# Window attention whose order is planned in Python: two step costs of the plan, and a new order of 281 offloaded tiles

## The chip, the cores and the metric

The kernel runs on one core of a Trainium2 chip. Its time is the device time of one execution in microseconds; the time of a kernel is the median of its runs. Five engines of the core work side by side, each through its own list of instructions: TensorE (PE in the profile, with its weight loads as PEld), ScalarE (ACT), VectorE (DVE), GpSimd (POOL) and SyncE (SP), which issues most DMAs. They wait for each other by semaphores only.

## The reference

An image of 224 x 224 positions with 96 channels (bf16) is projected to queries, keys and values. The first 48 channels attend within horizontal stripes of 8 rows, the other 48 within vertical stripes of 8 columns; a stripe has 8 x 224 = 1792 positions, and there are 28 stripes in each direction. The two halves are put side by side and projected by `wo`.

```
qkv = einsum('bhwc,cd->bhwd', x, wqkv)
# first 48 channels: 28 horizontal stripes of 1792 positions
ah = softmax(einsum('bqc,bkc->bqk', qh, kh) * 48 ** -0.5)
oh = einsum('bqk,bkc->bqc', ah, vh)
# last 48 channels: 28 vertical stripes, in the same way, give ov
return einsum('bhwc,cd->bhwd', concat(oh, ov), wo)
```

Nearly all of the work is the 1792 x 1792 scores of each of 56 stripes: their product, their exponential, and their product with the values.

## The kernel before

**Tiling.** Two stripes are worked on at once, in the two halves of TensorE's rows: 28 pairs P, first 14 horizontal, then 14 vertical. The 1792 queries of a pair are cut into four chunks c of 512, 512, 512 and 256. A tile is 128 keys of both stripes by the 512 queries of a chunk (in the last chunk 256 keys by 256 queries): 128 x 1024 scores in two PSUM banks. A pair has 14 + 14 + 14 + 7 = 49 tiles, the kernel 1372.

**The way of a tile.** Most tiles are ACT tiles: a score step on TensorE (`qk_fn`, matmuls on L670) writes two banks, ScalarE takes the exponential into a buffer PT (L888), and a value step on TensorE (`pv_fn`, L696) multiplies it with the values and sums in a bank per chunk. The others, here called offloaded tiles, get their exponential from DVE and POOL, by a square and a bit pattern. Their score step (`s_fn`, L683) goes to banks 6 and 7. In the short kind DVE moves the scores out (L1189), POOL squares them (L1105), TensorE computes the scores again (L683), and DVE combines both (L1199). In the long kind DVE copies once (L1188) and POOL does the rest (L1108 to L1111), with one score step. Which kind a tile becomes is decided by the planned backlog of POOL (L1187). ACT's score steps use the two bank pairs 0/1 and 2/3, and in some places the pair 6/7 as a third.

**Other work of TensorE.** Between these, TensorE projects keys and queries (L435) and values (L481) of the next pair, and finishes chunks: a finishing step (`fin_fills` from L513, matmuls on L530 for horizontal and L566 for vertical pairs) multiplies up to five blocks of 64 positions (or 128) with `wo`, and DVE and POOL scale and add.

**Two modes.** The planner distinguishes mode A (score steps of both kinds and finishing steps; contraction over 64 rows at most) from mode B (value steps and projections; contraction over 96 to 128 rows). Going from one to the other costs TensorE time.

**What sets the order.** No engine chooses anything at run time. `Sched` and the functions `step_pe`, `step_dve` and `step_pool` simulate the engines in Python while the program is built, with fixed costs from the top of the file (L25 to L35): a step of TensorE takes `D_MM` = 0.216 us, ACT comes every `P_ACT` = 0.9167 us, a change from A to B costs `SWT["AB"]` = 0.124 and from B to A 0.097. `commit` (L136) adds `W_PE` = 0.021 to the second step after a change; it keeps in `S.run` how many steps have followed the first of a run (0 for a lone step). `pe_switch` (L867) is the place where a change is charged; if the last step of mode A was a finishing step it adds `W_FIN`. The finishing steps are given 0.026 us for each of their n blocks (L547, L597). From these costs the planner knows at each moment how long it has until ACT's next score step is due (`slack` in `step_pe`), and puts value steps, projections, finishing and offloaded steps into it. The simulated order then becomes the engines' lists; `settle` (L1259) puts in the waits that are needed. So the costs change no instruction, only the order.

`HOW` (L43) holds choices for each pair: a string of three digits, the numbers of offloaded tiles in the first three chunks; a number that sets how early the next pair's projections are due; and four words of twelve hexadecimal digits, a word per chunk, which `RULES` (L75) reads as thresholds for `step_pe`, `step_dve` and the kinds of tile. The first digit, for one, is the number of value steps (`B1`, L1065) for which there must be room before the planner leaves mode A:

```
win = slack - SW_AB - SW_BA
nn = min(npv + (1 if fb else 0), int((win + how()[8]) / D_MM + 1e-6))
if nn >= B1 or ...
```

The eighth digit allows an ACT tile to take the third bank pair (L992).

Of the kernel before, what the change touches and what calls it, by code (L numbers as in the profile page):

```python
# [24 lines left out]
SWT = {"AB": 0.124, "AC": 0.124, "BA": 0.097, "CA": 0.10, "BC": 0.098, "CB": 0.108}  # L25
SW_AB, SW_BA = SWT["AB"], SWT["BA"]
D_ACT, P_ACT, M_ACT, SEMA = 0.904, 0.9167, 1.0175, 0.053
D_MM, L_MM, L_PV, L_FILL = 0.216, 0.465, 0.44, 0.215
W_PE, W_FIN = 0.021, 0.06
SEMD, SEMP, SELF, SEMX = 0.15, 0.12, 0.19, 0.05  # L30
D_P1, D_SQ, D_ADD = 1.14, 1.852, 0.0019
D_TS, D_TW = 1.125, 1.28
# [8 lines left out]


HOW = [  # L43
    ("023", 11, "242426002612 394226102014 324227102012 327227100012"),
    ("464", 7, "336319113442 331319113442 331319113442 335319113444"),
    ("323", 12, "521219112723 539418120834 539418120834 434418120234"),
    ("354", 10, "399238123332 399238123343 569429010920 569429110923"),
    ("334", 2, "383429102532 383429102532 383425102532 383135102532"),
    ("334", 9, "383135102932 546317021634 562226102334 5a7326002334"),
    ("342", 7, "5a7326102314 5a7325002311 568429003732 568429003730"),  # L50
    ("446", 5, "568429003733 433316102523 566439000041 566439000021"),
    ("233", 1, "475325003244 475325023241 475325123243 479325121243"),
    ("444", 0, "479325101243 479225101224 479225101221 479225101222"),
    ("224", 0, "479225100222 2a2327102823 2a5327102823 2a5317002823"),
    ("424", 3, "245217002823 245217002843 245217022843 245217020843"),
    ("544", 8, "381329000711 381329000911 247236022532 4a8425113033"),
    ("243", 4, "511318021714 511318021714 511318001724 4a5438023343"),
    ("444", 1, "4a5428023343 4a5436023343 312316012422 312336012422"),
    ("224", 6, "332236012422 372436010422 5a1219103932 521239103932"),
    ("334", 9, "521239002931 521239002932 421239002942 421239002942"),  # L60
    ("443", 2, "369428110343 369428110342 366425110342 273436003342"),
    ("343", 6, "273436001331 273436001423 273436001423 273336001422"),
    ("224", 9, "379316100602 358338000810 222419002813 222419002512"),
    ("342", 5, "232419002542 279339002241 279319002241 522136000512"),
    ("444", 10, "522438000513 3a2329000422 3a7119100312 453417001532"),
    ("443", 8, "453417021530 449415012722 489415012022 542214103644"),
    ("334", 9, "542214103641 388426102621 388426100622 201438102334"),
    ("334", 12, "201418103334 201418123333 466216100841 318216113541"),
    ("323", 2, "318217112542 218218112542 541117111741 5a9436000032"),
    ("333", 4, "5a9138000032 5a9138002032 333319101722 335319100722"),  # L70
    ("453", 11, "335119100722 5a6316122020 5a6315121020 5a6325101020"),
]
OFF = [[int(d) for d in k] + [0] for k, _, _ in HOW]
TAIL = [t for _, t, _ in HOW]
# [89 lines left out]
def bass_standalone__window_attn_cswin__vision_kernel(  # L164
# [27 lines left out]
    with es:  # L192
# [64 lines left out]
        S = Sched()  # L257
# [255 lines left out]
        def fin_fills(P, fs):  # L513
            b = P % 2
            fills = []
            if ph_of(P) == 0:
                m = P
                hw = WB // 2
                for bc0 in (list(range(0, hw, FS)) + list(range(hw, WB, FS)) if m == 0 else range(0, WB, FS)):
                    n = min(FS, (hw if m == 0 and bc0 < hw else WB) - bc0)  # L520
                    need = chunk_of_col((bc0 + n) * 64 - 1)
                    ri = rcn[0] % NRC
                    rcn[0] += 1

                    def pe_fn(e, bk, bc0=bc0, n=n):
                        bk3 = bk[:, 0:FS * (C + 1)].rearrange("p (s c) -> p s c", s=FS)
                        for s in range(n):
                            bc = bc0 + s
                            for w in range(2):
                                ins = e.matmul(bk3[64 * w:64 * w + 64, s, :],  # L530
                                               lhsT=o_of(P, w, bc),
                                               rhs=woh[64 * w:64 * w + CA, :], start=True, stop=True)
                        return ins

                    def d1(e, bk, n=n, ri=ri):
                        bk3 = bk[:, 0:FS * (C + 1)].rearrange("p (s c) -> p s c", s=FS)
                        return e.reciprocal(rc[ri][:, 0:n], bk3[:, 0:n, C])

                    def d2(e, bk, n=n, ri=ri, bc0=bc0):
                        bk3 = bk[:, 0:FS * (C + 1)].rearrange("p (s c) -> p s c", s=FS)  # L540
                        dst = Ph_sb[:, m, bc0:bc0 + n, :]
                        if m == 0:
                            v = bc0 // hw
                            dst = Ph_sb[:, m, :, :].rearrange("p (a v) c -> p v a c", v=2)[:, v, bc0 - v * hw:bc0 - v * hw + n, :]
                        return e.tensor_tensor(dst, bk3[:, 0:n, 0:C],  # L545
                                               rc[ri][:, 0:n].unsqueeze(2).to_broadcast([128, n, C]), ALU.mult)
                    fills.append((need, fill("A", 0.026 * n, pe_fn,  # L547
                                             ["wo"] + [("OT", b, c) for c in range(chunk_of_col(bc0 * 64), need + 1)],
                                             [(0.1, d1, [], [("rc", ri)], None),
                                              (0.06 + 0.104 * n, d2, [("rc", ri)], ["Ph"], None)],  # L550
                                             [("OT", P, need)], ("fin", P, bc0))))
            else:
                for w in range(2):
                    j = 2 * (P - NPH) + w
                    for k0 in range(0, NKT, fs):
                        n = min(fs, NKT - k0)
                        late = P == NP - 1 and k0 + n == NKT
                        need = chunk_of_col((k0 + n) * 128 - 1)
# [31 lines left out]
                        for s in range(n):  # L590
                            def d2(e, bk, s=s, ri=ri, w=w, kt=k0 + s, j=j):
# [2 lines left out]
                                                              Ph_sb[:, kt, j, :], ALU.mult, ALU.add)  # L594
                            chain.append((0.225, d2, [("rc", ri), "Ph"], [("o", P, w, k0 + s), ("out", P - 2)], None,
                                          (P, w, k0 + s, j)))
                        fills.append((need, fill("A", 0.026 * n, pe_fn,  # L597
                                                 ["wo"] + [("OT", b, c) for c in range(chunk_of_col(k0 * 128), need + 1)],
                                                 chain, [("OT", P, need), ("fin", NPH - 1, 25)], ("fin", P, w, k0))))
            return sorted(fills, key=lambda z: z[0])  # L600
# [112 lines left out]
        mode = ["B"]  # L713
# [117 lines left out]
        for need, f in fin_fills(0, FS):  # L831
            fin_q.append(f)
# [3 lines left out]
        fin_last = [False]  # L836
# [43 lines left out]
        def issue_qka(t, s):  # L880
            tl = act_seq[ia[0]]
            slot = slot_free.pop(0)
            t = pe_switch(t, "A")
            since[0] += 1
            fin_last[0] = False
            S.commit("pe", t, D_MM, L_MM, qk_fn(tl, s), kt_keys(tl), set_keys(s), fresh=set_keys(s),
                     tag=("qk", tl["P"], tl["c"], tl["kts"][0]))
            S.commit("act", 0.0, D_ACT, None, lambda e, s=s, slot=slot: e.activation(  # L888
                PT[slot][:], ps[:, 512 * SETS[s]:512 * SETS[s] + 1024], ACTF.Exp, scale=LN2 / 128.0),
                set_keys(s), pt_keys(slot), fresh=pt_keys(slot))  # L890
# [457 lines left out]
```

## Time and profile before

| | |
|---|---|
| median of 3 runs | 1017.95 us (1017.44 to 1018.09) |
| profiled execution, its own time | 1017.86 us |
| its span, first to last instruction | 1016.0 us |
| granted TensorE clock | 1.000 |
| exponentials on ACT (L888) | 1090 |
| tiles on DVE and POOL, short and long kind | 180 and 102 |
| busy: PE, ACT, POOL, DVE | 98%, 99%, 92%, 91% |

The span leaves out 1.9 us of the execution's own time ahead of the first and after the last instruction. Each matmul's time in the profile contains the time in which it passes through the array, so starts of successive steps, and not lengths, tell how long TensorE needs for one. ACT's instructions overlap in the same way: the distance of their starts is shorter than their length.

### The profile page before, as it was taken

The numbers are of one execution on the slowest core, as the hardware profiler recorded it, in microseconds if no ns is written. First come the engines' busy times: TensorE is split into PE (matmuls) and PEld (weight loads), VectorE is DVE, ScalarE is ACT, GpSimd is POOL, SyncE is SP. The second block draws the span as 40 slices with busy tenths as digits, with TensorE's granted clock in tenths as the row PEclk, the third lists the DMA queues.
The fourth block names the chain that finished last, engine by engine and source line by source line (L and its number), as shares of the span: only waits on it lengthen the run. The fifth ranks groups of instructions, "written<-read, shape, count | busy, mean of one in ns | idle before, by whom it ended". The sixth has DMA issues, their size and how long they took to land.

```text
span 1016.0 us, 31766 instructions
## 1 busy us (share of the span) xinstructions
PE 994.1 (98%) x13833; PEld 401.2 (39%) x13833; DVE 927.0 (91%) x1509; ACT 1005.9 (99%) x1101; POOL 931.8 (92%) x666
## 2 busy tenths in 40 slices
PE   9999999999999999999999999999999999999998
PEld 4434433433343344334334334333443433343343
DVE  7999899889998989899999999889999999999897
ACT  8999999999999999999999999999999999999997
POOL 5999999899999999998999999999889899999993
PEclk9999999999999999999999999999999999999999
DMA  4403203204202311220111221223313033313111
GB/s 87 98 28 65 67 14 65 66 2 79 65 2 65 79 34 34 65 38 13 28 38 23 56 54 25 51 57 65 53 20 62 18 59 55 61 21 57 24 21 37
DMA packets 162877, 47.08 MB, mean 46 GB/s; under 512 B 155895, under 2 KB 162711, under 8 KB 162738
## 3 DMA queue, kind: packets, MB, share of 16 engines
q1 hardware_dynamic: 161762, 44.59, 21.8%
q8 instruction: 108, 1.77, 0.7%
q10 hardware_dynamic: 976, 0.47, 0.2%
q14 instruction: 31, 0.25, 0.1%
HBM read 10.60 MB, written 19.28 MB: 29 GB/s over the span
## 4 chain that ended last, share of the span: by engine, by line
ACT 97%; PE 2%; DVE 0%; issue 0%; DVEq 0%
ACT PT L888 97%; PE ps L696 1%; PE ps L670 1%; PE ps L346 0%; ACT xT_sb L747 0%; PE ps L481 0%; PE ps L731 0%; DVE out_all L593 0%; PE ps L566 0%; PE ps L463 0%; DVE OT_sb L1164 0%; PE ps L435 0%; DVE warm L309 0%; DVE rc L573 0%; DVEq L192 0%
## 5 line engine op out<-in xcount | busy, mean ns | idle before, releaser
L888 ACT ACTIVATE PT<-ps 128x1024 bf16<-128x1024 f32 x1090 | 1001.5, 1078 | 1.3 <-PE ps L670 1.1
L670 PE MATMUL ps<-QT_sb,KT_sb 49*64 49x512 bf16 (+1 forms) x5144 | 446.0, 363 | 15.4 <-ACT PT L888 3.4
L696 PE MATMUL ps<-PT,V_sb 128*49 128x512 bf16 (+1 forms) x3136 | 451.5, 360 | 0.3 <-ACT PT L888 0.2
L1105 POOL TENSOR_TENSOR PT<-qb 128x1024 f16<-128x1024 f32 x180 | 337.8, 1893 | 8.8 <-DVE qb L1189 5.2
L670 PEld LDWEIGHTS ps<-QT_sb,KT_sb 49*64 49x64 bf16 x5144 | 129.3, 103 | 341.6 <-ACT PT L888 315.0
L1189 DVE TENSOR_SCALAR qb<-ps 128x1024 f32<-128x1024 uint16 x180 | 219.9, 1222 | 22.4 <-PE ps L683 20.1
L1199 DVE SCALAR_TENSOR_TENSOR PT<-ps,PT 128x1024 uint16<-128x1024 bf16 x180 | 219.7, 1221 | 17.3 <-PE ps L683 15.9
L696 PEld LDWEIGHTS ps<-PT,V_sb 128*49 128x49 bf16 x3136 | 134.7, 103 | 165.8 <-issue 130.2
L1109 POOL TENSOR_TENSOR PT<-PT 128x1024 f16<-128x1024 f16 x102 | 193.0, 1892 | 5.9
L683 PE MATMUL ps<-QT_sb,KT_sb 50*64 50x512 bf16 x1848 | 181.3, 382 | 1.3 <-DVE V_sb L488 0.2
L1110 POOL TENSOR_SCALAR qb<-PT 128x1024 uint16<-128x1024 f16 x102 | 137.4, 1347 | 8.8
L1108 POOL TENSOR_SCALAR PT<-qb 128x1024 f16<-128x1024 uint16 x102 | 106.5, 1044 | 33.0 <-DVE qb L1188 24.2
L1188 DVE COPY qb<-ps 128x1024 f32<-128x1024 f32 x102 | 124.6, 1221 | 7.9 <-PE ps L683 5.9
L1111 POOL TENSOR_SCALAR PT<-qb 128x1024 uint16<-128x1024 f32 x102 | 106.5, 1044 | 8.3
L451 DVE CAST QT_sb<-ps 128x512 bf16<-128x512 f32 (+1 forms) x111 | 67.6, 615 | 10.2 <-PE ps L435 9.9
L1164 DVE CAST OT_sb<-ps 113x512 bf16<-113x512 f32 x112 | 69.3, 618 | 5.7 <-PE ps L696 4.7
L440 DVE TENSOR_SCALAR_CACHE_REDUCE KT_sb<-ps 128x512 bf16<-128x512 f32 x108 | 65.9, 615 | 1.2 <-PE ps L435 0.6
L683 PEld LDWEIGHTS ps<-QT_sb,KT_sb 50*64 50x64 bf16 x1848 | 52.5, 104 | 33.3 <-DVE PT L1199 6.3
L545 DVE TENSOR_TENSOR Ph_sb<-ps,rc 128x480 bf16<-128x480 f32 (+1 forms) x84 | 52.4, 623 | 2.8
L488 DVE CAST V_sb<-ps 128x480 bf16<-128x480 f32 (+1 forms) x84 | 51.4, 619 | 3.3 <-PE ps L481 2.8
L584 POOL TENSOR_TENSOR out_all<-tmp,Ph_sb 128x480 bf16<-128x480 f32 (+1 forms) x48 | 49.8, 1046 | 3.2 <-DVE tmp L580 2.6
L593 DVE SCALAR_TENSOR_TENSOR out_all<-ps,rc,Ph_sb 128x96 bf16<-128x96 f32 x165 | 40.5, 310 | 1.1
(63 smaller groups left out, 416.2 us busy)
## 6 DMA issues: line engine op xcount, KB each, us to landing
cols_dram<-in_x_dram SPq DMA_DIRECT2D x28, 336.0 KB
out_dram<-out_all SPq DMA_DIRECT2D x387, 24.0 KB, 1.9
xT_sb<-cols_dram SPq DMA_TRANSPOSE x28, 4.6
xT_sb<-in_x_dram SPq DMA_TRANSPOSE x26, 4.6
xT_sb<-ones_dram SPq DMA_DIRECT2D x26, 7.0 KB
Ph_sb<-in_x_dram SPq DMA_DIRECT2D x2, 168.0 KB, 3.7
Ph_sb<-in_x_dram ACTq DMA_DIRECT2D x2, 168.0 KB, 3.9
out_dram<-out_all ACTq DMA_DIRECT2D x5, 24.0 KB, 1.9
```

The costliest lines, as they stand in the source:

```text
L670: ins = e.matmul(bank(SETS[s] + w)[64 * kh:64 * kh + 64, i * t["qs"]:(i + 1) * t["qs"]], lhsT=KT_sb[b][64 * w:64 * w + CA, kt * 128 + 64 * ...
L683: ins = e.matmul(bank(PB0 + w)[64 * kh:64 * kh + 64, 0:512], lhsT=KT_sb[b][64 * w:64 * w + nr, kt * 128 + 64 * kh:kt * 128 + 64 * kh + 64] ...
L696: ins = e.matmul(bank(pb)[64 * w:64 * w + CA, 0:t["qs"]], lhsT=V_sb[b][:, w, kt, :], rhs=PT[slot][:, ca:ca + t["qs"]], start=st and i == 0 ...
L888: S.commit("act", 0.0, D_ACT, None, lambda e, s=s, slot=slot: e.activation(PT[slot][:], ps[:, 512 * SETS[s]:512 * SETS[s] + 1024], ACTF.Ex ...
L1105: return [("pool", (D_SQ, L_SQ, 0.0), lambda e: e.tensor_tensor(y, q, q, ALU.mult), qk, yk)]
L1108: return [("pool", (D_TS, L_TS, LATE_TS), lambda e: e.tensor_scalar(y, lo, 2.0 ** -16, QH, ALU.mult, ALU.add), qk, yk), ("pool", (D_SQ, L_ ...
L1109: ("pool", (D_SQ, L_SQ, 0.0), lambda e: e.tensor_tensor(y, y, y, ALU.mult), yk + ["pser"], yk),
L1110: ("pool", (D_TW, L_TW, LATE_TS), lambda e: e.tensor_scalar(lo, y, 65536.0 * P2, 65536.0 * QC0, ALU.mult, ALU.add), yk + ["pser"], [("q", ...
L1111: ("pool", (D_TS, L_TS, LATE_TS), lambda e: e.tensor_scalar(bits, q, 1.0, 128.0 * (127.0 - SOFF), ALU.mult, ALU.add), qk, yk)]
L1188: S.commit("dve", t, D_P1, D_P1 + SEMD, lambda e: e.tensor_copy(qb[tl["qb"]][:], ps[:, PB0 * 512:(PB0 + 2) * 512]) if tl["whole"] else e.t ...
L1189: qb[tl["qb"]][:], ps[:, PB0 * 512:(PB0 + 2) * 512]) if tl["whole"] else e.tensor_scalar(
L1199: S.commit("dve", t, D_P1, D_P1 + SEMD, lambda e: e.scalar_tensor_tensor(PT[tl["slot"]][:].bitcast(U16), half(BF16, 1), 128.0 * (127.0 - S ...
```

## The change

It has three parts. The score steps of a run: `pe_switch` takes `W_RUN` = 0.0225 us off the cost of a change from A to another mode, if at least one step followed the first one of the run (`S.run` not 0). The finishing steps: each is given 0.03 us more, and `W_FIN` goes from 0.06 to 0.03, so that a finishing step followed by a change costs the same as before apart from `W_RUN`, and one followed by another step of mode A costs 0.03 more. The order: all 28 rows of `HOW` are new; their first strings add up to 281 offloaded tiles, where it was 282.

```diff
-W_PE, W_FIN = 0.021, 0.06
+W_PE, W_FIN, W_RUN = 0.021, 0.03, 0.0225
...
 HOW = [
-    ("023", 11, "242426002612 394226102014 324227102012 327227100012"),
-    ("464", 7, "336319113442 331319113442 331319113442 335319113444"),
...
-    ("453", 11, "335119100722 5a6316122020 5a6315121020 5a6325101020"),
+    ("032", 8, "4a2223101924 322438100622 496417100211 496417100241"),
+    ("335", 6, "496418100243 254318001934 254318001930 254318001930"),
...
+    ("444", 6, "332238101512 332238102512 305327102022 493114003041"),
 ]
...
-                    fills.append((need, fill("A", 0.026 * n, pe_fn,
+                    fills.append((need, fill("A", 0.026 * n + 0.03, pe_fn,
...
-                        fills.append((need, fill("A", 0.026 * n, pe_fn,
+                        fills.append((need, fill("A", 0.026 * n + 0.03, pe_fn,
...
         def pe_switch(t, m):
             if mode[0] == m:
                 return t
-            d = SWT[mode[0] + m] + (W_FIN if mode[0] == "A" and fin_last[0] else 0.0)
+            d = SWT[mode[0] + m] + (W_FIN if mode[0] == "A" and fin_last[0] else 0.0) - (W_RUN if mode[0] == "A" and S.run else 0.0)
```

More of the change, by code (lines that the diff above doesn't have):

```diff
@@ L43 @@
 HOW = [
-    ("023", 11, "242426002612 394226102014 324227102012 327227100012"),
-    ("464", 7, "336319113442 331319113442 331319113442 335319113444"),
[L46 to L70, printed above, removed]
-    ("453", 11, "335119100722 5a6316122020 5a6315121020 5a6325101020"),
+    ("032", 8, "4a2223101924 322438100622 496417100211 496417100241"),
@@ new lines @@
+    ("335", 6, "496418100243 254318001934 254318001930 254318001930"),
+    ("423", 12, "245427002132 245427002124 245427002621 245427002621"),
+    ("334", 10, "245127002622 245127102622 482427000343 482427000313"),
+    ("335", 12, "236128100724 236128000721 236328000731 236328000233"),
+    ("333", 8, "401237100624 401238102624 401228002624 369219101213"),
+    ("443", 10, "369119101213 368319101613 268339101611 268339101614"),
+    ("335", 6, "268329101614 268329101613 268329102621 228328102421"),
@@ new lines @@
+    ("333", 9, "282424001943 282427001943 282427002943 232427002941"),
+    ("535", 10, "232428002943 262418002643 269328100311 269228101333"),
+    ("322", 9, "209218101333 209218100333 209418101333 209418001333"),
+    ("535", 3, "251329102314 251329002314 251219002314 451219002314"),
+    ("324", 12, "4a6226120822 231228101544 231328102544 231328102644"),
+    ("334", 6, "557219112633 555219012633 555419012630 555119002631"),
+    ("324", 12, "585119001631 585119001632 585419001632 585219001632"),
@@ new lines @@
+    ("355", 2, "385219001532 385219001732 585219001232 587219001232"),
+    ("344", 8, "587219001234 431325000911 375335001012 279318101622"),
+    ("323", 5, "279418101622 454328002542 454428001542 454428001542"),
+    ("434", 7, "598218000832 598218000833 598218000833 2a1434110021"),
+    ("324", 10, "345219021641 245219021641 247319021642 463336002423"),
+    ("422", 10, "443236022423 365318112712 365318012722 365418012722"),
+    ("433", 11, "365415012742 334218102913 434218102913 434218002913"),
@@ L72 @@
+    ("424", 8, "225337110041 4a9217000642 4a9217000642 4a9217000642"),
+    ("345", 12, "4a9317002632 4a9317003632 4a9317003634 542428023242"),
+    ("323", 4, "542428003241 316218102911 3a6318102913 3a6318101913"),
+    ("532", 4, "3a6318101413 3a6318101513 3a6318001513 3a2318001743"),
+    ("444", 6, "3a2318001743 302218001743 302238101743 302238101613"),
+    ("444", 6, "332238101512 332238102512 305327102022 493114003041"),
 ]
```

## The prediction

> **What bounds the kernel now.** I began with the page: span, busy shares, the chain that ended last, and the groups. The columns of a group are line, engine, operation, tiles, shapes, count, then busy us, mean ns of one, idle us before them and what ended that.
>
> ```profile
> span 1016.0 us, 31766 instructions
> PE 994.1 (98%) x13833; PEld 401.2 (39%) x13833; DVE 927.0 (91%) x1509; ACT 1005.9 (99%) x1101; POOL 931.8 (92%) x666
> ACT 97%; PE 2%; DVE 0%; issue 0%; DVEq 0%
> L888 ACT ACTIVATE PT<-ps 128x1024 bf16<-128x1024 f32 x1090 | 1001.5, 1078 | 1.3 <-PE ps L670 1.1
> L1105 POOL TENSOR_TENSOR PT<-qb 128x1024 f16<-128x1024 f32 x180 | 337.8, 1893 | 8.8 <-DVE qb L1189 5.2
> L1189 DVE TENSOR_SCALAR qb<-ps 128x1024 f32<-128x1024 uint16 x180 | 219.9, 1222 | 22.4 <-PE ps L683 20.1
> L1199 DVE SCALAR_TENSOR_TENSOR PT<-ps,PT 128x1024 uint16<-128x1024 bf16 x180 | 219.7, 1221 | 17.3 <-PE ps L683 15.9
> L1109 POOL TENSOR_TENSOR PT<-PT 128x1024 f16<-128x1024 f16 x102 | 193.0, 1892 | 5.9
> L683 PE MATMUL ps<-QT_sb,KT_sb 50*64 50x512 bf16 x1848 | 181.3, 382 | 1.3 <-DVE V_sb L488 0.2
> L1110 POOL TENSOR_SCALAR qb<-PT 128x1024 uint16<-128x1024 f16 x102 | 137.4, 1347 | 8.8
> L1108 POOL TENSOR_SCALAR PT<-qb 128x1024 f16<-128x1024 uint16 x102 | 106.5, 1044 | 33.0 <-DVE qb L1188 24.2
> L1188 DVE COPY qb<-ps 128x1024 f32<-128x1024 f32 x102 | 124.6, 1221 | 7.9 <-PE ps L683 5.9
> L1111 POOL TENSOR_SCALAR PT<-qb 128x1024 uint16<-128x1024 f32 x102 | 106.5, 1044 | 8.3
> ```
>
> The kernel looks bound by ScalarE (ACT): its 1090 exponentials fill 1001.5 of 1016.0 us, and the chain gives ACT 97%. But one exponential lasts 1078 ns, and (1001.5 - 1.08) / 1089 gives one start per 0.9187 us: neighbours overlap by 0.16 us, so an exponential that comes up to 0.16 us late leaves no idle time and the page cannot show it. The timeline of ACT can (start, length, count):
>
> ```profile
> 538.76 12.95 ACT L888 ACTIVATE PT<-ps 128x1024 bf16<-128x1024 f32 x14
> 550.52 1.19 ACT L888 ACTIVATE PT<-ps 128x1024 bf16<-128x1024 f32 x1
> ...
> 244.31 1.05 ACT L888 ACTIVATE PT<-ps 128x1024 bf16<-128x1024 f32 x1
> 245.42 1.02 ACT L888 ACTIVATE PT<-ps 128x1024 bf16<-128x1024 f32 x1
> ```
>
> From 538.76 to 550.52 there are 13 starts, 0.9046 us apart: this is what ACT does when its scores are there. From 244.31 to 245.42 it took 1.11 us. Over the kernel 1089 x (0.9187 - 0.9046) = 15.4 us are such hidden lateness: ACT's floor is 1089 x 0.9046 = 985.1 us, and TensorE's order puts 15.4 on top. Who is late? The waits of the weight loads:
>
> ```profile
> PEld ps L670 <- ACT PT L888: 315.0, 875, 0.8
> PEld ps L696 <- issue: 130.2, 522, 0.4
> ```
>
> In 875 places a score step's weights waited for ACT to free its PSUM banks: TensorE is early there. The second row is time between score steps and value steps. So ACT and TensorE take turns as the bound: TensorE waits in most score steps, and in the rest ACT starts late. DVE and POOL are busy 91% and 92%.
>
> **The change, part by part.**
>
> *One tile goes back to ACT.* The first strings of the 28 rows of the order add up to 282 tiles for DVE and POOL before (the page: 180 + 102) and to 281 after; so 1091 exponentials. Cost: one start, 0.9046 us at the floor, 0.9187 at the mean. I take +0.92, since the other 1090 keep the mean too.
>
> *That tile leaves DVE, POOL and TensorE.* A tile of the short kind is two DVE passes (1.22 + 1.22) and one POOL square (1.89), and two score steps; of the long kind one DVE pass, 1.04 + 1.89 + 1.35 + 1.04 = 5.32 of POOL, and one score step. DVE and POOL stand 8 to 9% idle, beside ACT; I cost this at 0, the lower end is one score step's 0.24 us (timeline below, 92.33 to 92.58) twice, -0.5. If that cover were gone, with POOL the bound, it would be up to -5.3; POOL's 84 us of idle time speak against it.
>
> *The new prices.* They cost no instruction; they tell the planner how long TensorE takes, and so decide how much it puts between two score steps. The planner was charging 0.216 for a score step plus 0.124 for the change to value work = 0.340 after any score step, and 0.130 + 0.060 + 0.124 = 0.314 after a finishing step of five blocks. Now, after at least two steps of the score kind, 0.216 + 0.124 - 0.0225 = 0.3175, and 0.160 + 0.030 + 0.124 - 0.0225 = 0.2915. What TensorE does stands in its timeline. I counted all changes from 20 to 1000 us; below are the first and the last of three kinds: a run that ends in an offloaded tile's step (L683, 194 times), one that ends in an ACT tile's step (L670, 229, of them 208 like these), and one that ends in a finishing step of five (76).
>
> ```profile
> 23.65 0.39 PE L683 MATMUL ps<-QT_sb,KT_sb 50*64 50x512 bf16 x4
> 23.96 0.40 PE L696 MATMUL ps<-PT,V_sb 128*49 128x512 bf16 x2
> ...
> 996.67 0.39 PE L683 MATMUL ps<-QT_sb,KT_sb 50*64 50x512 bf16 x4
> 996.98 0.40 PE L696 MATMUL ps<-PT,V_sb 128*49 128x512 bf16 x2
> ...
> 20.36 0.41 PE L670 MATMUL ps<-QT_sb,KT_sb 49*64 49x512 bf16 x4
> 20.70 0.40 PE L696 MATMUL ps<-PT,V_sb 128*49 128x512 bf16 x2
> ...
> 999.06 0.41 PE L670 MATMUL ps<-QT_sb,KT_sb 49*64 49x512 bf16 x4
> 999.40 0.40 PE L696 MATMUL ps<-PT,V_sb 128*49 128x512 bf16 x2
> ...
> 38.96 0.39 PE L530 MATMUL ps<-woh,OT_sb 49*64 49x97 bf16 x10
> 39.27 0.40 PE L696 MATMUL ps<-PT,V_sb 128*49 128x512 bf16 x2
> ...
> 981.04 0.38 PE L566 MATMUL ps<-wov,OT_sb 49*64 49x97 bf16 x10
> 981.35 0.41 PE L696 MATMUL ps<-PT,V_sb 128*49 128x256 bf16 x4
> ```
>
> After L683 the value step starts 0.31 us later (0.3175 is right, 0.340 was too much). After these L670 it is 0.34: the old price was right, the new is too low by 0.0225. After five finishing blocks it is 0.31: again the old price was right, and the new is too low by 0.019. Why the two kinds of score step differ is seen where the run stands in full, beside a score step that is alone:
>
> ```profile
> 86.78 0.41 PE L670 MATMUL ps<-QT_sb,KT_sb 49*64 49x512 bf16 x4
> 87.12 0.40 PE L696 MATMUL ps<-PT,V_sb 128*49 128x512 bf16 x2
> ...
> 92.03 0.38 PE L696 MATMUL ps<-PT,V_sb 128*49 128x512 bf16 x2
> 92.33 0.41 PE L670 MATMUL ps<-QT_sb,KT_sb 49*64 49x512 bf16 x4
> 92.58 0.39 PE L683 MATMUL ps<-QT_sb,KT_sb 50*64 50x512 bf16 x4
> 93.06 0.41 PE L670 MATMUL ps<-QT_sb,KT_sb 49*64 49x512 bf16 x4
> 93.40 0.41 PE L435 MATMUL ps<-xT_sb,w_sb 97*64 97x512 bf16 x2
> ```
>
> An unbroken second step starts 0.24 after the first and is left after 0.31 to 0.32: two cost 0.56, one alone 0.34, so the second adds one step's 0.216 and the change costs the same as after one. The L670 at 93.06 came 0.48 after the L683, not 0.24: it had waited, TensorE had run empty, and it is left like a lone step, after 0.34.
>
> So the prices do three things. (a) Right price, 194 x 0.0225 = 4.4 us: before, this was slack that the plan did not know of; now the plan can fill it. It is a gain for the order only as far as TensorE is the late one: between 0 and -4.4, and I take the middle, -2.2. (b) Too low, 208 x 0.0225 = 4.7 us: value work is planned that early and comes later: 0 to +4.7. These changes stand behind a score step that waited for ACT, where TensorE was early a moment ago, so I take less than the middle, a third, +1.6. (c) Too low after finishing steps, 76 x 0.019 = 1.4: 0 to +1.4, the middle, +0.7. The finishing step's own +0.03 is for those followed by another step of the score kind; there the 0.0225 comes off one step later, 0.0075 are left, and I cost that at nothing; at 53 places it would be 0.4 in either direction.
>
> The Trainium skill, TensorEngine Tiling (Array Packing), Key Properties, says that changing the tiling mode, not just the tile, drains TensorE. By that rule a change would cost the same whatever ran before it. The rows agree for unbroken runs (0.56 against 0.34, one step more) and the rule speaks against a price that depends on the length of the run; what it would make of the sum is the last rival below.
>
> *The new order.* All 28 rows are other choices. The trace of before cannot price them. Bounds: no order goes below ACT's floor (-15.4), and above it the sum has no end in the rows; nearest is the present order, value 0. I read from the strings: the value steps at which the planner leaves score work fall from a mean of 3.58 to 3.13, and the third pair of PSUM banks is allowed to ACT's tiles in 15 of 112 rows instead of 42.
>
> **Sum:** 0.92 - 2.2 + 1.6 + 0.7 = +1.0 us on the profiled execution's 1017.86 (span 1016.0), 1018.9. The median of the runs shown, 1017.95, is 0.1 above it, so the predicted time is 1019.0. Since 0.2% is about what a measurement of this kernel can tell from no change, "same" here is 1015.9 to 1020.0.
>
> **Rivals.**
>
> *The right price pays in full (faster).* All of (a) is won, (b) and (c) vanish in waits for ACT: 0.9 - 4.4 = -3.5, 1014.5. For it: the 875 waits, where TensorE has time; 15.4 us of lateness to take from. Against: it has to win the extra tile back first, so lateness must fall from 15.4 to under 12.4 before it counts as faster.
>
> *More changes between the kinds of work (slower).* A lower bound for leaving score work means more and shorter runs. A pair of changes costs 0.34 - 0.216 = 0.124 one way; the way back is 92.33 - 92.03 - 0.216 = 0.084; together 0.21 us. At half on the path, each added pair is +0.11; from 10 added pairs on, with the +1.0, it is slower by over 0.2%; 25 more (3% of the 790 changes that I counted in that stretch, 263 after a lone step among them) give +3.8, 1021.7. For it: cheaper changes invite it, and TensorE is 98% busy. Against: fewer offloaded tiles, hence one or two score steps less.
>
> *The prices do nothing.* The order is fixed by the strings; the prices shift no step much: only the tile stays, +0.92, 1018.9. It lies within the forecast.
>
> *A change costs the same after every run (slower).* Then 0.0225 is too little after all 194 + 208 + 76 = 478 runs, 10.8 us, half of it on the path: 0.9 + 5.4 = +6.3, 1024.2. This is the drain rule read strictly. The 0.31 after 23.65 and 996.67 speak against it.
>
> **How the numbers follow.** Forecast 0.41 and "the prices do nothing" 0.13, both same; right price in full 0.13, faster; more changes 0.30 and equal changes 0.03, slower. So faster 0.13, same 0.54, slower 0.33. The forecast's own range, with (a) or (b) moved by a quarter of its span (1.1 to 1.2 us), is 1017.8 to 1020.2. To leave out no more than 2 in 10, the range goes down to 1015.4, into the faster case, and up to 1022.2, over most of the case of more changes.
>
> **What would show it.** ACT: 1091 exponentials; a pitch of 0.9187 or a little above is the forecast, under 0.915 is the right price, 0.921 and more the slower cases. TensorE: 0.31 after L683 and 0.34 after an L670 that waited, as now; a changed number here would overturn (a) or (b). More places in the row of L696's loads on "issue" than 522 would show more changes. I am wrong if POOL or DVE, not TensorE, turn out to be what ACT's lateness hangs on, through value steps that wait for offloaded tiles, or if the new order itself, which I set at 0, is better or worse by more than the prices.

## The result and the profile after

The changed kernel takes 1020.36 us (median of 9 runs, 1020.09 to 1020.78), the kernel before 1018.02 on the same chip: ratio 1.0025, 95% interval [1.0017, 1.0034]. That is 1.4 us above the forecast of 1019.0 and just above the forecast's own range of 1017.8 to 1020.2. It lies inside the whole range on record, 1015.4 to 1022.2, which had been drawn wider to take in two rivals. With +2.3 us it is just beyond the 0.2% up to which the forecast said "same", and the interval has that bound in it.

The page of the kernel after (columns as before):

```profile
span 1018.4 us, 31719 instructions
...
PE 991.8 (97%) x13820; PEld 402.9 (40%) x13820; DVE 917.6 (90%) x1468; ACT 1008.1 (99%) x1102; POOL 948.1 (93%) x683
...
ACT 96%; PE 3%; DVE 0%; issue 0%; DVEq 0%
...
L888 ACT ACTIVATE PT<-ps 128x1024 bf16<-128x1024 f32 x1091 | 1003.8, 1067 | 1.4 <-PE ps L670 1.1
...
L1105 POOL TENSOR_TENSOR PT<-qb 128x1024 f16<-128x1024 f32 x177 | 332.3, 1892 | 6.7 <-DVE qb L1189 3.4
...
L1109 POOL TENSOR_TENSOR PT<-PT 128x1024 f16<-128x1024 f16 x104 | 196.8, 1892 | 6.6
```

There are 1091 exponentials and 177 + 104 = 281 offloaded tiles. One start takes (1003.8 - 1.07) / 1090 = 0.9199 us, it was 0.9187. The rows for exponentials grew by 2.3 us: 0.92 is the tile, 1.4 is lateness spread over all starts. TensorE is busy for 2.3 us less than before and the kernel is slower, so the sum of TensorE's work does not explain the difference; what is left to ask is when its score steps come.

The last exponentials, in the timeline of ACT, before and after (the first row is of two instructions):

```profile
1008.83 2.09 ACT L888 ACTIVATE PT<-ps 128x1024 bf16<-128x1024 f32 x2
```
```profile
1011.80 1.17 ACT L888 ACTIVATE PT<-ps 128x1024 bf16<-128x1024 f32 x1
```

They end at 1010.92 and 1012.97: 2.0 of the 2.4 us of span arise up to there, 0.4 after it.

TensorE's timeline of the kernel after, with the last change behind an offloaded tile's step (127 of them from 20 to 1000 us), the first behind an ACT tile's step that had waited (256), and the first behind five finishing blocks (62):

```profile
998.73 0.39 PE L683 MATMUL ps<-QT_sb,KT_sb 50*64 50x512 bf16 x4
999.05 0.40 PE L696 MATMUL ps<-PT,V_sb 128*49 128x512 bf16 x2
...
21.78 0.41 PE L670 MATMUL ps<-QT_sb,KT_sb 49*64 49x512 bf16 x4
22.12 0.40 PE L696 MATMUL ps<-PT,V_sb 128*49 128x512 bf16 x2
...
38.54 0.39 PE L530 MATMUL ps<-woh,OT_sb 49*64 49x97 bf16 x10
38.85 0.40 PE L696 MATMUL ps<-PT,V_sb 128*49 128x512 bf16 x2
```

0.32, 0.34 and 0.31: as in the kernel before. The chip has not changed its prices; the plan has.

**The planner's clock.** Since the order comes from a simulation in the kernel's code, that code has a time for the last exponential as well. It is no measurement, but beside the trace it tells how wrong the prices are in sum. Below, a trace whose last exponential ends before that time is called early, and one that ends after it late. Before, the clock says 1012.22 us and the trace 1010.92: 1.3 early. After, it says 1011.07 and the trace 1012.97: 1.9 late. The distance grows evenly and not in lumps: the first exponential of the kernel after is 0.9 us early, the 500th is on time, the last 1.9 late. So the new plan is 1.15 us better than the old one on paper, with a tile more on ACT, and it loses 3.2 us against its paper. The experiments ask what these 3.2 us are.

### The profile page after: what moved, and what is told of

It reads as the page before. It is cut to its first block, busy times and chain, and to the rows that moved or that the text cites. A ratio compares the mean times of both kernels' runs of the same rounds, so it can differ in the third digit from the quotient of the medians.

```text
span 1018.4 us, 31719 instructions
## 1 busy us (share of the span) xinstructions
PE 991.8 (97%) x13820; PEld 402.9 (40%) x13820; DVE 917.6 (90%) x1468; ACT 1008.1 (99%) x1102; POOL 948.1 (93%) x683
## 4 chain that ended last, share of the span: by engine, by line
ACT 96%; PE 3%; DVE 0%; issue 0%; DVEq 0%
ACT PT L888 95%; PE ps L696 1%; PE ps L670 1%; PE ps L346 0%; ACT xT_sb L747 0%; DVE out_all L593 0%; PE ps L435 0%; PE ps L683 0%; PE ps L463 0%; DVE OT_sb L1164 0%; PE ps L566 0%; PE ps L731 0%; PE ps L1095 0%; PE ps L481 0%; DVE warm L309 0%
## 5 line engine op out<-in xcount | busy, mean ns | idle before, releaser
L888 ACT ACTIVATE PT<-ps 128x1024 bf16<-128x1024 f32 x1091 | 1003.8, 1067 | 1.4 <-PE ps L670 1.1
L696 PE MATMUL ps<-PT,V_sb 128*49 128x512 bf16 (+1 forms) x3136 | 459.7, 361 | 0.0
L1105 POOL TENSOR_TENSOR PT<-qb 128x1024 f16<-128x1024 f32 x177 | 332.3, 1892 | 6.7 <-DVE qb L1189 3.4
L1189 DVE TENSOR_SCALAR qb<-ps 128x1024 f32<-128x1024 uint16 x177 | 216.2, 1221 | 21.9 <-PE ps L683 19.4
L1199 DVE SCALAR_TENSOR_TENSOR PT<-ps,PT 128x1024 uint16<-128x1024 bf16 x177 | 216.0, 1220 | 21.0 <-PE ps L683 18.4
L696 PEld LDWEIGHTS ps<-PT,V_sb 128*49 128x49 bf16 x3136 | 139.0, 103 | 174.4 <-issue 139.2
L1109 POOL TENSOR_TENSOR PT<-PT 128x1024 f16<-128x1024 f16 x104 | 196.8, 1892 | 6.6
L1110 POOL TENSOR_SCALAR qb<-PT 128x1024 uint16<-128x1024 f16 x104 | 139.9, 1345 | 9.0
L1188 DVE COPY qb<-ps 128x1024 f32<-128x1024 f32 x104 | 126.9, 1220 | 10.7 <-PE ps L683 9.4
L584 POOL TENSOR_TENSOR out_all<-tmp,Ph_sb 128x480 bf16<-128x480 f32 (+1 forms) x60 | 60.7, 1022 | 2.0 <-DVE tmp L580 0.8
L481 PEld LDWEIGHTS ps<-w_sb,xT_sb 96*64 96x64 bf16 x1568 | 37.8, 112 | 9.2 <-issue 1.6
```

The lines of the kernel that those rows point to most:

```text
L696: ins = e.matmul(bank(pb)[64 * w:64 * w + CA, 0:t["qs"]], lhsT=V_sb[b][:, w, kt, :], rhs=PT[slot][:, ca:ca + t["qs"]], start=st and i == 0 ...
L1105: return [("pool", (D_SQ, L_SQ, 0.0), lambda e: e.tensor_tensor(y, q, q, ALU.mult), qk, yk)]
L1109: ("pool", (D_SQ, L_SQ, 0.0), lambda e: e.tensor_tensor(y, y, y, ALU.mult), yk + ["pser"], yk),
L1110: ("pool", (D_TW, L_TW, LATE_TS), lambda e: e.tensor_scalar(lo, y, 65536.0 * P2, 65536.0 * QC0, ALU.mult, ALU.add), yk + ["pser"], [("q", ...
L1188: S.commit("dve", t, D_P1, D_P1 + SEMD, lambda e: e.tensor_copy(qb[tl["qb"]][:], ps[:, PB0 * 512:(PB0 + 2) * 512]) if tl["whole"] else e.t ...
L1189: qb[tl["qb"]][:], ps[:, PB0 * 512:(PB0 + 2) * 512]) if tl["whole"] else e.tensor_scalar(
```

## The experiments

### What the slack of the old prices was worth, and what lateness behind ACT tiles costs

In both kernels the order is left as it is, and 54 columns of one matmul of a step are computed a second time, ahead of the step's last matmul: in the kernel before in steps of offloaded tiles that end a run (195), in the kernel after in steps of ACT tiles that end a run (286).

```diff
+        for i in range(1, len(pe_log) - 1):
+            if pe_log[i] and pe_log[i][0] in ('s1', 's2') and in_a(pe_log[i - 1]) and not in_a(pe_log[i + 1]):
+                d, fn, inc = S.ops["pe"][i]
+                S.ops["pe"][i] = (d, lambda e, fn=fn: fn(e, 54), inc)
```

(in the second kernel `('qk',)` for `('s1', 's2')`).

> The kernel before, in its own order, with about 0.023 us added to each score step of an offloaded tile (L683) that ends an unbroken run: 54 columns of one of its four matmuls are computed twice, which at 0.216 us for 512 columns is an estimate of 0.0228. So 194 changes (counted from 20 to 1000 us) take 0.340 instead of 0.3175, the price that the old plan had for them: the slack of term (a) is taken away. My theory, half of it on the path: 194 x 0.0228 x 0.5 = +2.2 us. If waits for ACT hide it: 0. If TensorE is late everywhere: +4.4.

> The kernel after, in its own order, with the same 0.0228 us added to each score step of an ACT tile (L670) that ends a run of two or more, in some 279 places: what a lateness of 0.0225 behind these steps costs, the mispricing of term (b), is doubled. My theory, a third on the path: 279 x 0.0228 / 3 = +2.1 us on the kernel after (1022.5). If these steps always have time, because they stand behind a wait for ACT: 0 (1020.4). If all of it counts: +6.4 (1026.7).

The timelines of TensorE of the first and of the second, the added matmul in the row before the last:

```profile
23.35 0.39 PE L690 MATMUL ps<-QT_sb,KT_sb 50*64 50x512 bf16 x4
23.57 0.18 PE L688 MATMUL ps<-QT_sb,KT_sb 50*64 50x54 bf16 x1
23.68 0.40 PE L703 MATMUL ps<-PT,V_sb 128*49 128x512 bf16 x2
```
```profile
25.40 0.41 PE L674 MATMUL ps<-QT_sb,KT_sb 49*64 49x512 bf16 x4
25.64 0.18 PE L671 MATMUL ps<-QT_sb,KT_sb 49*64 49x54 bf16 x1
25.76 0.40 PE L703 MATMUL ps<-PT,V_sb 128*49 128x512 bf16 x2
```

The added matmul costs less than was estimated: the median from the step to the value step went from 0.318 to 0.333 and from 0.340 to 0.355, 0.015 each. The first kernel takes 1019.99 us beside 1017.65: ratio 1.0024 [1.0014, 1.0033], so 195 x 0.015 = 2.9 us of added time cost 2.3. But more than half of that lies behind the exponentials. Here are the last exponential of its profiled execution, and one of SyncE's last issues of output:

```profile
1010.53 1.16 ACT L895 ACTIVATE PT<-ps 128x1024 bf16<-128x1024 f32 x1
```
```profile
1012.92 2.06 SPq L272 DMA_DIRECT2D out_dram<-out_all  x1
```

This execution's span is 2.0 us longer than that of the kernel before. Its last exponential ends at 1011.69, 0.8 us later (1.1 later if the time is counted from the first exponential, which came sooner here). The other 1.2 us lie behind it, where no step has an added matmul (the last one is at 997.7) and where the issue shown took 2.06 us and its neighbours 0.6. So up to the last exponential 0.8 to 1.1 of the 2.9 us count, a quarter to a good third, and that the whole time came out near the +2.2 that I had expected is luck. The second kernel takes 1021.60: ratio 1.0040 [1.0027, 1.0054] to the kernel before, where the kernel after has 1.0025; the difference of the two is 1.5 us, that of the two spans (1019.5 and 1018.4) 1.1, and its last exponential ends 1.1 later, at 1014.06. Of 286 x 0.015 = 4.3 us a quarter to a third counts. So the two weights are much alike, and not a half and a third as the prediction had them. But the slack of the old prices was not idle: part of it was in use.

### One tile

```diff
-    ("453", 11, "335119100722 5a6316122020 5a6315121020 5a6325101020"),
+    ("353", 11, "335119100722 5a6316122020 5a6315121020 5a6325101020"),
```

> The kernel before with one digit changed: in the last pair 3 instead of 4 offloaded tiles in the first chunk, so 281 in all and 1091 exponentials, and the order of the 27 pairs before is as it was. Theory: one start of ACT more, +0.92 us, 1018.9. Rivals: the end of the kernel hides it, DVE or POOL being the last there, 0; or a tile less for these engines is worth more than it costs ACT, below 0.

The page's row of this kernel:

```profile
L888 ACT ACTIVATE PT<-ps 128x1024 bf16<-128x1024 f32 x1091 | 1002.4, 1078 | 1.3 <-PE ps L670 1.1
```

0.9 us more than before, and 1018.78 us beside 1017.74, ratio 1.0010 [1.0001, 1.0019]. The tile costs its start of ACT; what DVE and POOL save is worth nothing here.

### Other orders from the old and from the new prices

Strings were searched anew by one and the same search, once with the prices of before and once with those of after. Nothing else differs from those kernels.

> The kernel before with its own prices and an order of my own search (1091 exponentials). By the planner's own clock, which the code computes while it is built, the last exponential ends at 1014.65 us; in the kernel before that clock says 1012.22 and the trace 1010.93, in the kernel after 1011.07 and 1012.96. Theory (the prices decide how far the execution falls behind its plan): an order from the old prices ends early by 1.3 us again, 1013.3, so some 1020.5 us in all. Rival (the new order is one with bad luck, the prices have no part): the difference between clock and trace has nothing to do with the prices, and may be +1.9 as well, 1016.5, 1023.7 in all.

> The kernel after with its own prices and another order, of the same search with the same effort as for the old prices (1089 exponentials). By the planner's own clock the last exponential ends at 1013.93 us. Theory (the new prices are too low behind a score step that waited and behind finishing steps): the trace ends late by 1.9 us as in the kernel after, 1015.8, some 1022.2 us in all with the 6.4 us that lie between that end and the time of an execution by the plan. Rival (bad luck of one order): early by 1.3 as in the kernel before, 1012.6, 1019.0 in all.

The last exponential of each, in the timeline of ACT:

```profile
1012.03 1.18 ACT L888 ACTIVATE PT<-ps 128x1024 bf16<-128x1024 f32 x1
```
```profile
1015.64 1.03 ACT L888 ACTIVATE PT<-ps 128x1024 bf16<-128x1024 f32 x1
```

They end at 1013.21, 1.4 us ahead of the clock, and at 1016.67, 2.7 us behind it. So in these two pairs of orders the distance goes with the prices and not with the order. (In all the two take 1022.54 us, ratio 1.0058 [1.0044, 1.0073], and 1027.15, 1.0095 [1.0081, 1.0108]: the clock's own end is later there, and more is left behind the last exponential than I had allowed for.)

### Which price

Three searches with repaired prices. The first takes all from the traces:

```diff
-W_PE, W_FIN, W_RUN = 0.021, 0.03, 0.0225
+W_PE, W_FIN, W_RUN, W_BA = 0.021, -0.0065, 0.0225, 0.018
...
+            if max([start, self.free[eng]] + [self.when(eng, x) for x in d]) > self.pend + 0.05 and self.run:
+                self.run = 0
...
-                    fills.append((need, fill("A", 0.026 * n + 0.03, pe_fn,
+                    fills.append((need, fill("A", 0.0435 * n, pe_fn,
...
-            d = SWT[mode[0] + m] + (W_FIN if mode[0] == "A" and fin_last[0] else 0.0) - (W_RUN if mode[0] == "A" and S.run else 0.0)
+            d = SWT[mode[0] + m] + (W_FIN if mode[0] == "A" and fin_last[0] else 0.0) + (0.0 if mode[0] == "A" and not S.run else W_BA if mode[0] == "B" and not S.run else -W_RUN if mode[0] == "A" else 0.0)
```

The second repairs only the price behind steps that waited (`if S.run and not S.waited`), the third only the finishing steps (0.0435 n, `W_FIN` = -0.0065).

> The kernel after with prices of TensorE as the traces show them, and an order of the same search for them (1091 exponentials): 0.0225 comes off a change only if the last step of the run had not waited, a step that waited begins a run anew, a finishing step of n blocks takes 0.0435 n with nothing added at its change, the change from value to score work costs 0.018 more after a lone step, a value projection 0.0315 a block. By the planner's own clock the last exponential ends at 1013.99 us. Theory: TensorE's prices being right and ACT's (0.9167 a start against 0.9046 at the floor) still too high, the trace ends early, by 1 to 3 us: 1011 to 1013, in all 1018 to 1020 us. Rival (bad luck of orders): late or early by chance, as late as 1016.7 as in the order for the new prices.

> The kernel after with one price repaired, that of term (b): 0.0225 comes off a change only if the last step of the run had not waited; finishing steps keep the new prices. An order of the same search (1089 exponentials); by the planner's own clock the last exponential ends at 1017.64 us. In the two orders from the new prices the trace ended 1.9 and 2.7 us later than this clock. Theory: (b) makes most of that, 256 x 0.0225 x 0.37 (the share that the padded steps of ACT tiles showed) = 2.1 us, so here the trace is late by 0 to 0.6: 1017.6 to 1018.2. Rival: finishing steps make most of it, then still 1.5 to 2.5 late, 1019.1 to 1020.1.

> The kernel after with the other price repaired, that of term (c): a finishing step of n blocks takes 0.0435 n, with nothing added at its change; 0.0225 still comes off every change after two or more steps. An order of the same search (1090 exponentials); by the planner's own clock the last exponential ends at 1020.38 us. Theory: finishing steps make the smaller part, 0.5 to 1 us, so the trace is still late by 1 to 2 us: 1021.4 to 1022.4. Rival: they make most of it, and the trace is late by 0 to 0.6: 1020.4 to 1021.0.

The last exponential of the first, the second and the third:

```profile
1011.84 1.12 ACT L892 ACTIVATE PT<-ps 128x1024 bf16<-128x1024 f32 x1
```
```profile
1018.54 1.13 ACT L892 ACTIVATE PT<-ps 128x1024 bf16<-128x1024 f32 x1
```
```profile
1022.48 1.10 ACT L888 ACTIVATE PT<-ps 128x1024 bf16<-128x1024 f32 x1
```

The first is 1.0 us early (1012.96), as expected, though in all it took 1022.50 us and not 1018 to 1020. The second is 2.0 late, where its rival had 1.5 to 2.5. The third is 3.2 late, more than its theory or its rival had. But 1.2 us of this came in one place, where ACT stood still at times and the granted clock fell (us, then the busy times of PE, PEld, DVE, ACT, POOL, the granted clock and DMA):

```profile
930.00:956.00 26.00, 22.56 (x294) 8.43 (x292) 22.40 (x31) 17.91 (x20) 20.72 (x15) 0.87 0.08 15
```

Up to 930 us the third was 1.8 late, as its theory had it. So with either of the two blamed prices repaired, an order was still late by about 2 us, and the theory that (b), with some of (c), makes all of the 3.2 us falls; that they make a part of it does not. (The three take 1022.50, 1032.18 and 1033.42 us, ratios 1.0048 [1.0033, 1.0064], 1.0143 [1.0129, 1.0157], 1.0161 [1.0147, 1.0175].)

What the first repairs beside these two prices is the way back: from a value step that was alone to a score step. In the kernel before, behind a lone value step:

```profile
23.96 0.40 PE L696 MATMUL ps<-PT,V_sb 128*49 128x512 bf16 x2
24.29 0.41 PE L670 MATMUL ps<-QT_sb,KT_sb 49*64 49x512 bf16 x4
```

This takes 0.33 (the median over 222 places is 0.332), and both kernels' plans give it 0.216 + 0.097 = 0.313. Behind a run of value steps its median is 0.312 (92.03 to 92.33 in the prediction's rows is such a place). It is the same effect as on the way out, and the old prices were wrong on both sides with opposite signs: 194 x 0.0225 = 4.4 us too much, 222 x 0.018 = 4.0 us too little.

### The second theory: two errors that cancelled

The right part of the change alone (the old prices, and 0.0225 off behind an unbroken run that ends in a score step), its mirror (the old prices, and 0.018 more for the lone way back), and a second order from the traces' prices, by another seed:

```diff
+            d = SWT[mode[0] + m] + (0.0 if mode[0] != "A" else W_FIN if fin_last[0] else -W_RUN if S.run and not S.waited else 0.0)
...
+            d = SWT[mode[0] + m] + (W_FIN if mode[0] == "A" and fin_last[0] else 0.0) + (0.018 if mode[0] == "B" and not S.run else 0.0)
```

> The part of the change that the trace of before bears out, alone: the prices of before, with 0.0225 off a change only behind an unbroken run that ends in a score step; finishing steps as before. An order of the same search (1089 exponentials); by the planner's own clock the last exponential ends at 1018.52 us. New theory: the old prices held two errors that cancelled, 0.0225 too much after such runs and 0.018 too little for the way back to score work after a lone value step; this kernel repairs the first alone, and has 310 such ways back, 5.6 us too little. Orders whose errors cancel ended 1.0 to 1.4 us ahead of the clock; about a third of a net error became lateness. So here +0.3 to +1.5 us late, the last exponential ends at 1018.8 to 1020.0. Rival: the way back has no part in it, the harm is in the ACT tiles' and the finishing steps' prices alone; then 1.0 to 1.4 us early, 1017.1 to 1017.5.

> The mirror of it: the prices of before, with 0.018 added to the way back to score work after a lone value step, and the 0.0225 too much after runs left in. An order of the same search (1089 exponentials); by the planner's own clock the last exponential ends at 1028.74 us. New theory: 213 runs that end in an offloaded tile's step are 4.8 us too dear, a third of it is won: 2 to 3.5 us early, 1025.2 to 1026.7. Rival: the way back has no part, 1.3 us early as with the prices of before, 1027.4.

> A second order from the prices that the traces show, of a search with another seed (1088 exponentials); by the planner's own clock the last exponential ends at 1014.45 us. Theory (right prices give the same distance whatever the order): 0.7 to 1.4 us early, 1013.0 to 1013.8, in all about 1022. Rival (the distance is a matter of the order): anything between 1.5 early and 3 late.

The last exponential of the first and of the third:

```profile
1018.80 1.11 ACT L892 ACTIVATE PT<-ps 128x1024 bf16<-128x1024 f32 x1
```
```profile
1012.55 1.03 ACT L892 ACTIVATE PT<-ps 128x1024 bf16<-128x1024 f32 x1
```

The first ends at 1019.90, 1.4 late, within what the second theory said and far from its rival's 1017.5. The third ends at 1013.58, 0.9 early, within its bounds, but the kernel took 1029.48 us and not about 1022. The mirror was a miss as a whole: it ended at 1037.3, 8.6 us late. Its busy times in three windows (columns as above) show where:

```profile
0.00:778.00 778.00, 761.40 (x10541) 306.26 (x10541) 694.05 (x1121) 773.41 (x848) 730.13 (x531) 1.00 0.24 48
778.00:860.00 82.00, 75.33 (x920) 27.86 (x916) 65.68 (x109) 65.78 (x71) 67.76 (x48) 0.88 0.16 28
860.00:1046.90 186.90, 175.53 (x2354) 70.63 (x2350) 164.19 (x293) 168.97 (x183) 158.65 (x111) 0.96 0.20 38
```

From 778 us on its order has holes, in which the granted clock fell; the planner fills some holes with idle matmuls, but its costs are those of the full clock throughout. From the first to the 800th exponential, ahead of the holes, the trace had gained 1.2 us on the planner's clock, against 0.6 in the kernel before and 0.5 in the other order from the old prices. That is the expected direction, but as a test of the whole it stays inconclusive. The three take 1030.18, 1048.71 and 1029.48 us, one execution each, beside 1017.44.

The orders together, by the net error of their prices (counts from 20 to 1000 us, x 0.0225 behind runs, x 0.018 for the lone way back, x 0.019 behind five finishing blocks; plus is too little). The last column leaves out the distance at the first exponential, which is 0.1 to 0.9 us early in these traces and differs between executions of one order too: in the three kernels that begin with the order of the kernel before it is 0.5 to 0.8 us early.

| order | net error of the prices, us | last exponential, trace against clock, us | the same, from the first exponential on |
|---|---|---|---|
| before | 222 x 0.018 - 194 x 0.0225 = -0.4 | -1.3 | -0.8 |
| old prices, other order | 347 x 0.018 - 282 x 0.0225 = -0.1 | -1.4 | -1.1 |
| traces' prices, two orders | 0 | -1.0, -0.9 | -0.4, -0.7 |
| run price alone | 298 x 0.018 = 5.4 | +1.4 | +1.8 |
| waited steps repaired | 332 x 0.018 + 86 x 0.019 = 7.6 | +2.0 | +2.5 |
| finishing steps repaired | 249 x 0.018 + 198 x 0.0225 = 8.9 | +3.2 | +4.1 |
| after | 137 x 0.018 + 256 x 0.0225 + 62 x 0.019 = 9.4 | +1.9 | +2.8 |
| new prices, other order | 274 x 0.018 + 162 x 0.0225 + 85 x 0.019 = 10.2 | +2.7 | +3.2 |

In the row of the finishing steps, 1.2 us are the place at 930 us; without them it has +2.9 in the last column, and the column follows the net error to a few tenths. The mirror is not in the table, for its holes. With no net error the chip is about a microsecond ahead of the plan (ACT's floor is 0.9046 and the plan has 0.9167); of a net error some four tenths become lateness: from -1.1 to +2.6 over the last three rows' mean of 9.5, an estimate from one trace an order. In the kernel after, 5.8 of the 9.4 us are term (b), 1.2 term (c) and 2.5 the lone way back.

### A tenth of a nanosecond

```diff
-W_PE, W_FIN, W_RUN = 0.021, 0.03, 0.0225
+W_PE, W_FIN, W_RUN = 0.021, 0.03, 0.0224
```

> The kernel after with W_RUN = 0.0224 in place of 0.0225, and its strings as they are. By the planner's own clock the last exponential then ends at 1047.06 instead of 1011.07 us: the strings fit one set of prices to the tenth of a nanosecond. Theory (the prices choose the order): the execution follows, 1047 to 1050 for the last exponential and some 1055 to 1060 us in all. Rival of the prediction, that the prices do nothing because the strings fix the order: 1020.4.

1069.84 us, beside 1017.44 of the kernel before: the prices choose the order, and strings that were found for one set of prices do not serve for one that is a tenth of a nanosecond away. The last exponential ended at 1060.3, 13 us behind the clock, where I had given it 3 at most. Its windows:

```profile
0.00:660.00 660.00, 644.16 (x8947) 262.02 (x8949) 588.05 (x911) 654.81 (x719) 608.80 (x444) 1.00 0.23 48
660.00:1067.00 407.00, 376.61 (x4946) 150.85 (x4940) 334.07 (x568) 356.38 (x384) 339.57 (x240) 0.95 0.22 38
```

Again the loss against the clock comes with the holes: it is 1.1 us up to 660 us, and the rest comes behind, with a granted clock of 0.95.

## Why the prediction was right, and where it was not

**What bounds the kernel** was read rightly: ACT and TensorE in turns, with the lateness hidden in ACT's overlap. Up to the last exponential the difference is the tile's start and ACT's pitch of 0.9199, where the forecast had "0.9187 or a little above", less the 0.4 us by which the first exponential ended sooner. The sign of being wrong that names DVE and POOL did not come: the weight loads of value steps waited for a PT from these engines for 2.6 us in 10 places before and for 2.6 in 10 after.

**The tile, +0.92,** and nothing for DVE and POOL: right. The kernel with one tile moved measured 0.9 on ACT and 1.0 in all.

**The prices as read from TensorE's timeline** were right for the score steps, and stayed what they were. Behind five finishing blocks the 0.31 of the rows stands for 0.317 in horizontal pairs and 0.310 in vertical ones, so (c) was 1.7 us rather than 1.4. The weights were a middle of (a) and a third of (b); up to the last exponential the padded kernels showed a quarter to a good third for both.

**The sum** had -2.2 for the order's gain and +1.6 and +0.7 for lateness. On the planner's clock the gain is 1.15 with the tile in it, so 1.15 + 0.92 = 2.1 without it. That this is close to the 2.2 of (a) is luck: it is the gain of an order that was searched anew. In the other pair of orders the new prices gained nothing on paper: the clock says 1013.93 in place of 1014.65, but for two exponentials fewer, which are 1.8 us of ACT. The lateness came out at 3.2 instead of 2.3, and 0.4 us were added behind the last exponential. These 1.3 us are the miss: 0.92 - 2.1 + 3.2 + 0.4 = 2.4 against +1.0. It is the wider range, kept for rivals that did not come, that holds the result.

**The step that failed** is in (a): "before, this was slack that the plan did not know of; now the plan can fill it." It was not free. In the old prices it made up in sum for the lone way back, which the plan has 0.018 too cheap. The prediction had the two rows for a way back (92.03 and 92.33), took the 0.084 + 0.216 of a run of value steps for all of them, and never compared a lone one. With it the terms of lateness would have had 0.3 to 0.4 of another 2.5 to 4 us, about +1, and the forecast would have been 1020. That repairing the score steps' price alone makes an order late was shown in one order (1.4 late, against 1.3 and 1.4 early with both errors in place); its mirror was not shown cleanly.

**The rivals.** "The right price pays in full" and "a change costs the same after every run" did not come: 0.32 stayed behind 998.73. The Trainium skill, TensorEngine Tiling (Array Packing), Key Properties, has a change of mode drain TensorE. The trace agrees in that every change costs time, once for an unbroken run: 0.240 + 0.318 for two steps and 0.340 for one, 0.218 apart; a draining as such no row shows. "More changes" was wrong in its sign: 730 changes from A to B in place of 790, 137 lone value steps in place of 222; the lower bound for leaving score work went with longer runs of value steps. The sign given for it did not serve: the row of L696's loads rose from 522 places on "issue" to 578,

```profile
PEld ps L696 <- issue: 139.2, 578, 0.4
```

while the changes became fewer; the row of L435's loads fell from 83 to 30 at the same time. The time that it gave for the slower side, 1021.7, came near for another reason. "The prices do nothing" fell with a tenth of a nanosecond. Of the 0.4 us more behind the last exponential, 0.2 lie ahead of the last piece of output that DVE writes (2.5 us behind the last exponential before, 2.7 after), and the rest mostly in the issues of output that follow; why was not tried.

**No version beats the kernel before.** The two orders from the traces' prices took 1022.50 and 1029.48 us; their lateness was repaired, but their plans were no better than the old one, and they took 7.4 and 14.1 us behind the last exponential, where the kernel before takes 5.1.

## What to carry to other kernels

When a plan is corrected from a trace, compare every price in it with the trace before one is changed: two wrong ones may cancel, and the correction of one can then be a loss. Judge such a change by the distance between the plan's time and the measured one over several orders, not by one new order's time. And where an engine's instructions overlap, read its lateness from the distance of starts: the page's idle column showed 1.4 us of some 17.

## What the runs showed of the hardware that was not expected

The first step after a change is the dear one on both sides: 0.34 for a lone score step against 0.318 behind a run, and 0.332 for a lone value step against 0.312. A matmul of 54 columns, computed again within a step, put off the next step by 0.015 us and not by the 0.0228 that its columns would take.

Where TensorE ran short of work, its granted clock went to a half. In the second order from the traces' prices, the end of the kernel (columns as in the windows above) ran

```profile
1000.00:1013.90 13.90, 12.59 (x170) 4.58 (x168) 11.24 (x17) 13.58 (x15) 13.40 (x10) 1.00 0.15 30
1010.50:1013.90 3.40, 2.23 (x36) 0.72 (x28) 2.37 (x3) 3.08 (x4) 3.31 (x3) 1.00 0.17 34
1013.90:1027.60 13.70, 6.77 (x71) 4.18 (x69) 5.17 (x15) 0.00 (x0) 4.08 (x5) 0.50 0.15 29
```

at 0.50 for 13.7 us, after 3.4 us in which TensorE was busy for 2.23. The kernel before needs 5.1 us from its last exponential to its end. How much of the difference is the clock's was not separated: this order also has 71 matmuls left in that stretch, and the kernel before 19.
